# Another step order, other engines for some copies and other PSUM banks in a recurrent-attention and token-mixing kernel

## The chip, the cores and the metric

The kernel runs on one core of a Trainium2 chip. The time is device microseconds of one execution. Engines are named as in the profile: PE does matrix multiplies (PEld its weight loads), DVE, ACT and POOL work elementwise, SP issues the loads and stores. Each engine takes its instructions strictly in the order in which the program lists them, and an instruction waits until the steps that it depends on are done.

## The reference

Two stages follow each other. The first is a recurrence over 768 tokens, for 4 batches and 8 heads of width 48, with a decay `w` per token and channel; the second mixes the tokens of each batch by a matrix made from two projections, applies a relu and a last projection.

```python
for t in range(S):
    cur = np.einsum('bhd,bhe->bhde', u[None] * kt, vt)
    y[:, :, t] = np.einsum('bhd,bhde->bhe', rt, state + cur)
    state = wt[:, :, :, None] * state + np.einsum('bhd,bhe->bhde', kt, vt)
...
W_tok = scale * np.einsum('bsd,btd->bst', x @ w_q, x @ w_k)
mixed = np.einsum('bst,btd->bsd', W_tok, x)
return (np.maximum(mixed, 0.0) @ w_out).astype(np.float32)
```

Inputs and output are float32; `x` is the first stage's result, 4 x 768 x 384.

## The kernel before

The 3072 tokens are cut into 12 units of 256 (three to a batch), and each unit into two chunks of 128. Steps carry the unit's number and, where there are two, the chunk's: AM.8.1 is the second chunk of unit 8. A unit goes through these steps (in brackets the engines that may take one):

- Loads (SP): wg, kg, rg, vg, 384 KB each, into rings of four buffers; for the last batch v comes in four parts, vw. SP then also issues the stores, st.
- ln (ACT) takes the logarithm of the decay into lw, k16, r16 and v16 (POOL, ACT or DVE) cast k, r, v to bf16. On PE cw sums the logarithms along the tokens, kT and rT transpose k and r into one PSUM tile, vp reorders v. In PSUM they are read by ep and en (ACT: exponentials of the sum and of its negative), ks (a copy of the transposed k), VB (a copy of v; in the last batch straight from vw).
- RT (DVE) is r times ep, KT is k times en. KT has three forms: on POOL or DVE from the copy ks (way P or D, line 526), or on DVE straight from PSUM (way d, line 521). qT (DVE) is r times k; dps (PE) and dd make from it the current token's own share, and Vd (POOL or DVE, line 575) is VB times dd.
- A (PE) is the product of KT and RT per head, AM (DVE, line 595) masks it on its way out of PSUM. kb (PE) transposes KT back, kd copies it, sn (PE) forms the new state, SB (DVE) scales it. yi and ya (PE) give the output from the state and from AM and VB, and X (DVE, lines 710 and 715) adds Vd.
- xt, XT transpose X; qk and QK make the unit's queries and keys (in unit 11 they are split in wk, wq, wkc, wqc). When a batch is complete, T (PE) sums keys times X, TS copies it; then for each of the batch's units mx (PE), rl (relu into MX), fp (PE, the last projection), os (a copy out of PSUM) and st.

Units 0 and 11 do several steps in halves. Before unit 0, `setup` writes constants and masks and has PE do 18 multiplies of zeros, Z; twelve more such multiplies, z, lie among the steps. pads sets the unused columns of the two kd buffers to zero, uC, uT and UB bring the bonus `u` into place.

Nothing here is ordered by a scheduler. Class `Plan` only collects the 734 steps with their dependencies; `order` then reads three tables. `ORDER` (line 82) is a permutation of the steps' numbers: the program is written out in that order, and each engine gets its own steps in that order. `WAYS` (line 124) has a letter for each step that allows several, and picks the engine or the form; `BANKS` (line 129) gives the PSUM bank (of eight; a wide tile takes two) of each tile that lies there. A step that fills a bank waits until the bank's last reader is done.

```python
for s in self.steps:
    if len(s["ways"]) > 1:
        s["way"] = next(ways)
    s["eng"] = self.ENGINE[s["way"]]
for b, x in zip(self.banks, BANKS):
    b.bank = x
for i in ORDER:
    ...
```

Letters in `WAYS`: A, D and P are ACT, DVE and POOL, d is KT's PSUM form on DVE, and E, e and c are forms of a PE step: whole transposes or ones in 64-row halves, and a state product in two column halves (c).

Of the kernel before, what the change touches and what calls it, by code (L numbers as in the profile page):

```python
# [32 lines left out]
class Plan:  # L33
# [89 lines left out]
]  # L123
WAYS = (
    "PDDDAPPDDdPADPPDDEEEAAPPAdPAAPEAcEEAAPPAPPADPeDEEDAAAAAAAAPPDPDADPeAcEEDAPPAdPAAPEAEEEDA"
    "PPDPPAAPeAEEAAAAAAAAAAPDPPAAPEDEcEAAPPDPPDAPEAEEEAAPPDPPAAPeDceAAAAADADDPAAPPAPEDcEEDAPP"
    "DPPAPeAcceAAPPDPPPAPPAEEDDAEDADAAADAAAADADDA"
)
# [765 lines left out]
```

## Time and profile before

| | |
|---|---|
| runs | 100.68, 101.51, 102.75 us; median 101.51 |
| span of the profiled execution, first to last instruction | 99.6 us |
| instructions | 4492 |
| moved by DMA | 24.68 MB, mean 248 GB/s |
| granted PE clock | 1.00 |

The profiled execution's own time is its span and what lies before the first and after the last instruction; the trace shows only the span. The lowest of the three runs is 1.1 us over it, the median 1.9 us.

In a row of a timeline the first number is the start from the span's beginning, the second the time from the start of a group's first instruction to the end of its last, in us; brackets name the idle time of the engine before it and what ended that. In a row of the groups, `x8 | 17.4, 2169 | 2.3 <-` says eight instructions, 17.4 us busy, 2169 ns on average, 2.3 us of idle time before them and what ended it. Neighbours on one engine overlap by some 0.08 us, so means add up to a little more than busy time.

### The profile page before, as it was taken

Reading aid. Unit: us, or ns where it says so; the run is one execution under the profiler, and the core shown is the slowest. Engines: PE = TensorE matmul, PEld = TensorE weight load, DVE = VectorE, ACT = ScalarE, POOL = GpSimd, SP = SyncE. Lnnn points to the kernel's source line nnn. Section 1 sums busy time; section 2 is a strip of 40 time slices with the busy share of each in tenths; the row PEclk is TensorE's granted clock in tenths of the full one; section 3 lists DMA queues with packets and bytes.
Section 4 is the critical chain, followed back from the end, with each engine's and each line's share of the span. In section 5 each row is a group of like instructions: output and inputs, shape, how many; then the busy total and the mean of one; then the engine's idle time right before and its main releaser. Section 6 shows DMA issues by size and latency. Waiting matters only on the chain.

```text
span 99.6 us, 4492 instructions
## 1 busy us (share of the span) xinstructions
PE 86.6 (87%) x1906; PEld 63.3 (64%) x1911; DVE 84.9 (85%) x154; ACT 79.0 (79%) x135; POOL 69.5 (70%) x82
## 2 busy tenths in 40 slices
PE   5978796879886998999999999889998999999930
PEld 1325473756774767777776777759787687776610
DVE  6284999799979999979999999999999799783740
ACT  6034998799996799899999998999899766666920
POOL 6866354999799895799999989498996392500000
PEclk9999999999999999999999999999999999999999
DMA  1999999799999999999999977998993056030794
GB/s 17 313 327 349 324 337 296 195 295 335 289 314 298 225 311 329 344 321 268 271 330 305 316 114 218 251 156 201 282 417 115 7 210 264 10 158 7 277 367 149
DMA packets 45141, 24.68 MB, mean 248 GB/s; under 512 B 31552, under 2 KB 43968, under 8 KB 45120
## 3 DMA queue, kind: packets, MB, share of 16 engines
q1 hardware_dynamic: 44960, 24.19, 84.0%
q8 instruction: 15, 0.25, 0.9%
q10 hardware_dynamic: 160, 0.20, 0.5%
q14 instruction: 6, 0.05, 0.1%
HBM read 19.66 MB, written 4.72 MB: 245 GB/s over the span
## 4 chain that ended last, share of the span: by engine, by line
PE 37%; DVE 23%; SPq 20%; DMA 7%; issue 7%; ACT 3%; ACTq 0%; DVEq 0%
PE PS L179 37%; SPq L232 9%; SPq L237 8%; DMA vg<-in_v_dram 7%; DVE AM L595 7%; DVE X L710 6%; DVE RT L516 3%; SPq L355 2%; DVE qT L506 2%; DVE ks L333 2%; DVE SB L658 1%; ACT VB L327 1%; SPq L357 1%; ACT MX L339 1%; DVE kd L335 1%
## 5 line engine op out<-in xcount | busy, mean ns | idle before, releaser
L595 DVE TENSOR_TENSOR AM<-PS,US 128x1024 bf16<-128x1024 f32 x24 | 28.8, 1218 | 0.7 <-PE PS L179 0.7
L526 POOL TENSOR_TENSOR KT<-ks,en 128x1024 bf16<-128x1024 bf16 (+1 forms) x10 | 19.7, 1965 | 4.7 <-DVE ks L333 3.3
L575 POOL TENSOR_TENSOR Vd<-VB,dd 128x768 bf16<-128x768 bf16 (+1 forms) x14 | 18.1, 1293 | 4.5 <-ACT dd L327 3.4
L454 ACT ACTIVATE en<-PS 128x1024 bf16<-128x1024 f32 (+1 forms) x14 | 12.5, 907 | 3.0 <-PE PS L179 2.9
L179 PEld LDWEIGHTS <-KT 48*128 48x128 bf16 (+1 forms) x312 | 9.7, 94 | 6.6 <-issue 4.5
L447 ACT ACTIVATE ep<-PS 128x512 bf16<-128x512 f32 (+1 forms) x28 | 13.7, 555 | 0.1
L179 PE MATMUL PS<-wo,MX 128*128 128x384 bf16 x72 | 13.5, 327 | 0.0
L710 DVE SCALAR_TENSOR_TENSOR X<-PS,gx,Vd 128x384 bf16<-128x384 f32 x22 | 12.5, 609 | 0.7 <-PE PS L179 0.6
L407 ACT ACTIVATE lw<-wg 128x768 bf16<-128x768 f32 x12 | 10.3, 857 | 2.9 <-DMA wg<-in_w_dram 2.9
L179 PE MATMUL PS<-RT,KT 48*128 48x128 bf16 x192 | 9.7, 218 | 1.2 <-ACT VB L327 0.4
L327 ACT COPY os<-PS 128x768 f32<-128x768 f32 (+1 forms) x11 | 7.9, 714 | 3.5 <-PE PS L179 3.5
L418 POOL CAST k<-kg 128x768 bf16<-128x768 f32 x10 | 8.3, 827 | 2.5 <-DMA kg<-in_k_dram 2.5
L179 PE MATMUL PS<-Z 128*128 128x512 bf16 x25 | 8.4, 461 | 1.4 <-DVE Z L250 1.2
L418 POOL CAST r<-rg 128x768 bf16<-128x768 f32 x10 | 8.2, 825 | 1.6 <-DMA rg<-in_r_dram 1.6
L179 PEld LDWEIGHTS <-MX 128*128 128x128 bf16 x72 | 6.5, 97 | 3.6 <-DVE MX L341 0.2
L516 DVE TENSOR_TENSOR RT<-PS,ep 128x1024 bf16<-128x1024 bf16 (+1 forms) x14 | 8.4, 605 | 0.0
L179 PE MATMUL PS<-VB,AM 128*128 128x48 bf16 x192 | 8.0, 184 | 0.4 <-issue 0.4
L506 DVE TENSOR_TENSOR qT<-PS,ks 128x1024 bf16<-128x1024 bf16 x12 | 8.2, 684 | 0.1
L339 ACT ACTIVATE MX<-PS 128x768 bf16<-128x768 f32 (+1 forms) x12 | 8.0, 682 | 0.4
L179 PE MATMUL PS<-CM,lw 64*128 64x128 bf16 x192 | 7.4, 217 | 0.5 <-DVE AM L595 0.3
L327 ACT CAST VB<-PS 128x768 bf16<-128x768 f32 x8 | 6.4, 804 | 1.1 <-PE PS L179 0.6
L179 PEld LDWEIGHTS <-AM 128*128 128x128 bf16 x192 | 6.3, 96 | 1.6 <-issue 0.7
(90 smaller groups left out, 191.9 us busy)
## 6 DMA issues: line engine op xcount, KB each, us to landing
kg<-in_k_dram SPq DMA_DIRECT2D x12, 384.0 KB, 6.4
wg<-in_w_dram SPq DMA_DIRECT2D x12, 384.0 KB, 5.0
rg<-in_r_dram SPq DMA_DIRECT2D x12, 384.0 KB, 5.8
vg<-in_v_dram SPq DMA_DIRECT2D x9, 384.0 KB, 6.3
out_dram<-os SPq DMA_DIRECT2D x9, 384.0 KB, 2.5
vw<-in_v_dram SPq DMA_DIRECT2D x4, 288.0 KB, 6.7
out_dram<-os SPq DMA_DIRECT2D x5, 192.0 KB, 2.4
wof<-in_moe_w_out_dram SPq DMA_DIRECT2D x1, 576.0 KB, 6.2
```

The lines of the kernel that those rows point to most:

```text
L179: return nc.tensor.matmul(o, l, rr, start=start, stop=stop, skip_group_check=True, is_transpose=trans)
L327: nc.scalar.copy(o, i)
L407: nc.scalar.activation(view(lw.tile, 0, [[64, H], [512, 2], [1, D]]), view(g["wg"].tile, 0, [[D2, H], [D, 2], [1, D]]), ACT.Ln, bias=0.0, ...
L418: op(view(o.tile, 0, [[64, NP], [256, 4], [1, D]]), view(g[src].tile, 0, [[2 * D2, NP], [D, 4], [1, D]]))
L447: nc.scalar.activation(view(ep.tile, cs[0] * NP * EW + off, [[EW, NP * len(cs)], [step, 2], [1, 32]]), view(at(cw), cs[0] * 512 + j * 64, ...
L454: nc.scalar.activation(en.tile[:, ds(cs[0] * 512, w_)], at(cw)[:, ds(cs[0] * 512, w_)], ACT.Exp, bias=0.0, scale=-1.0)
L506: lambda e: nc.vector.tensor_tensor(plain(qT.tile), turned(512), plain(ks.tile), ALU.mult),
L516: nc.vector.tensor_tensor(plain(RT.tile, cs, 32), turned(512, cs, True), plain(ep.tile, cs, EW // 4), ALU.mult)
L526: x.tensor_tensor(KT.tile[:, cols], ks.tile[:, cols], en.tile[:, cols], ALU.mult)
L575: (nc.vector if e == "D" else nc.gpsimd).tensor_tensor(Vd.tile[:, cols], VB.tile[:, cols], view(dd.tile, cs[0] * H, [[1, len(cs) * H], [0, ...
L595: AMs[c] = add(("AM", n, c), "D", lambda e, c=c, A=A: nc.vector.tensor_tensor(view(AM[c].tile, 0, [[C, 8], [1, C]]), view(at(A), 0, [[C, 8 ...
L710: nc.vector.scalar_tensor_tensor(view(X.tile, 2 * i * DM + hh * D, [[D2, H], [1, D]]), view(at(y), hh * 512, [[D, H], [1, D]]), gx, view(V ...
```

## The change

All three tables are replaced; no other line is touched. Every step of before is there after, with the same dependencies.

```diff
 ORDER = [
-    0, 3, 13, 2, 21, 22, 23, 15, 16, 17, 1, 24, 25, 26, 27, 28, 29, 76, 77, 78, 31, 73, 74, 75,
+    0, 1, 2, 3, 4, 14, 13, 15, 16, 17, 18, 19, 30, 33, 73, 74, 75, 20, 85, 35, 37, 21, 22, 23,
...
 WAYS = (
-    "PDDDAPPDDdPADPPDDEEEAAPPAdPAAPEAcEEAAPPAPPADPeDEEDAAAAAAAAPPDPDADPeAcEEDAPPAdPAAPEAEEEDA"
+    "PPDADPPDdPPAAPPDDccEADPPAPAAAPEDcEEDAPPAdPADPEAceAAAAAAAAAPADPPADPeAEcEDAPPAdPAADeAEceDA"
...
 BANKS = [
-    7, 2, 0, 6, 0, 6, 4, 4, 1, 1, 6, 6, 5, 4, 2, 6, 0, 0, 0, 7, 7, 6, 4, 5, 4, 4, 2, 2, 7, 0, 0,
+    3, 0, 6, 0, 7, 4, 6, 0, 5, 4, 6, 4, 5, 4, 2, 6, 4, 6, 0, 5, 5, 6, 2, 4, 4, 2, 0, 2, 3, 0, 0,
...
```

Of the elementwise steps, these change their engine. To DVE: UB, QK.0, QK.10, XT.1, TS.8, TS.11, Vd.4, dd.6, dd.11, kd.1, kd.7, KT.2, KT.11 (both halves, in form d), wqc.11.0, os.6, os.9.1, and the relus rl.9 (both halves), rl.10.0 and rl.11.0. From DVE to ACT: uC, dd.0, XT.2, XT.9, XT.11.0, kd.2, kd.8, VB.7, ks.11, rl.7, rl.8, rl.11.1, os.8, os.9.0, os.10.1, os.11.0. Between POOL and the others: pads.0, KT.0.1, KT.1, v16.3, k16.6 and r16.9 come to POOL, v16.1 and r16.3 go from it to ACT. KT.0's first half stays on DVE and takes form d. On PE 18 steps change their form.

SP's first loads are wg.0, wg.1, kg.0, rg.0, kg.1, vg.0 in place of kg.0, wg.0, rg.0, vg.0, kg.1, wg.1; later wg.3 stands ahead of the weights, and vg.3 ahead of kg.4 and behind wg.4; wg.11 ahead of kg.11.

The first place is POOL's queue from its first cast on. Names are those of the buffers, so KT_0 and Vd_0 hold the even units. Before:

```order
L421 CAST k16_0_89<-kg_0_71 128x8x2x48
L421 CAST r16_0_87<-rg_0_67 128x8x2x48
L333 CAST v16_0_103<-vg_0_75 128x8x2x48
L418 CAST k16_1_90<-kg_1_72 128x4x4x48
L418 CAST r16_1_88<-rg_1_68 128x4x4x48
L333 CAST v16_1_104<-vg_1_76 128x8x2x48
L575 TENSOR_TENSOR Vd_0_109<-VB_0_105,dd_0_107 128x384
L418 CAST k16_0_89<-kg_2_73 128x4x4x48
L575 TENSOR_TENSOR Vd_0_109<-VB_0_105,dd_0_107 128x384
```

After:

```order
L297 MEMSET kd_0_83 128x64
L298 MEMSET kd_0_83 128x16x80
L421 CAST k16_0_89<-kg_0_71 128x8x2x48
L421 CAST r16_0_87<-rg_0_67 128x8x2x48
L526 TENSOR_TENSOR KT_0_101<-ks_0_95,en_0_93 128x512
L418 CAST k16_1_90<-kg_1_72 128x4x4x48
L333 CAST v16_0_103<-vg_0_75 128x8x2x48
L418 CAST r16_1_88<-rg_1_68 128x4x4x48
L526 TENSOR_TENSOR KT_1_102<-ks_1_96,en_1_94 128x1024
L575 TENSOR_TENSOR Vd_0_109<-VB_0_105,dd_0_107 128x384 x2
L418 CAST k16_0_89<-kg_2_73 128x4x4x48
```

A pad, half of KT.0 and all of KT.1 have come in; v16.1 has left; both halves of Vd.0 stand behind KT.1 and ahead of k16.2.

The second place is DVE's queue around the two steps that read only SBUF. Before, in unit 3, from the masked second chunk of unit 2 on:

```order
L595 TENSOR_TENSOR AM1_0_113<-PS_62,US_146 128x1024
L333 COPY ks_1_96<-PS_62 128x1024
L658 TENSOR_TENSOR SB_0_115<-PS_62,ep_0_91 128x192
L333 CAST v16_1_104<-vg_3_78 128x8x2x48
L506 TENSOR_TENSOR qT_1_98<-PS_62,ks_1_96 128x1024
L516 TENSOR_TENSOR RT_1_100<-PS_62,ep_1_92 128x1024
L710 SCALAR_TENSOR_TENSOR X_0_125<-PS_62,gx_150,Vd_0_109 128x8x48 x2
```

After, in unit 5, from ks.5 on:

```order
L333 COPY ks_1_96<-PS_62 128x1024
L506 TENSOR_TENSOR qT_1_98<-PS_62,ks_1_96 128x1024
L658 TENSOR_TENSOR SB_0_115<-PS_62,ep_0_91 128x192
L516 TENSOR_TENSOR RT_1_100<-PS_62,ep_1_92 128x1024
L575 TENSOR_TENSOR Vd_0_109<-VB_0_105,dd_0_107 128x768
L595 TENSOR_TENSOR AM0_0_111<-PS_62,US_146 128x1024
L595 TENSOR_TENSOR AM1_1_114<-PS_62,US_146 128x1024
```

The cast of v.3 has left DVE's queue; the product Vd.4, which was POOL's, stands ahead of the masks of units 4 and 5.

The third place is the end of DVE's queue, from the first half of X.11 on. Before:

```order
L715 SCALAR_TENSOR_TENSOR X_1_126<-PS_62,gx_150,Vd_1_110 128x384 x2
L333 COPY XT_1_120<-PS_62 128x384
L333 COPY XT_0_119<-PS_62 128x384
L333 CAST QK_1_128<-PS_62 128x64
L341 TENSOR_SCALAR MX_3_124<-PS_62 128x768
L341 TENSOR_SCALAR MX_0_121<-PS_62 128x768
L333 CAST QK_1_128<-PS_62 128x128
L333 COPY os_0_79<-PS_62 128x768
L333 COPY os_1_80<-PS_62 128x384
L341 TENSOR_SCALAR MX_3_124<-PS_62 128x3x128
L333 COPY os_2_81<-PS_62 128x384
L333 COPY os_3_82<-PS_62 128x384
```

After:

```order
L715 SCALAR_TENSOR_TENSOR X_1_126<-PS_62,gx_150,Vd_1_110 128x384
L333 COPY os_2_81<-PS_62 128x768
L715 SCALAR_TENSOR_TENSOR X_1_126<-PS_62,gx_150,Vd_1_110 128x384
L333 COPY XT_0_119<-PS_62 128x384
L333 CAST QK_1_128<-PS_62 128x64
L333 CAST QK_1_128<-PS_62 128x384
L333 CAST QK_1_128<-PS_62 128x128 x2
L333 CAST TS_1_130<-PS_62 128x384
L341 TENSOR_SCALAR MX_1_122<-PS_62 128x3x128
L341 TENSOR_SCALAR MX_2_123<-PS_62 128x3x128
L341 TENSOR_SCALAR MX_3_124<-PS_62 128x3x128
L341 TENSOR_SCALAR MX_1_122<-PS_62 128x3x128
```

os.6 stands between the halves of X.11, the relus of units 9 to 11 follow TS.11, and one more row, a copy os_1 of half of unit 9, ends the queue. On PE the order behind T.11 was fp.7, mx.9, fp.8, mx.10, fp.9, mx.11, fp.10, fp.11 and is fp.8, mx.9, mx.10, mx.11, fp.9.0, fp.10, fp.11, fp.9.1, with fp.7 ahead of T.11.

More of the change, by code (lines that the diff above doesn't have):

```diff
@@ L82 @@
 ORDER = [
[40 rows of a table removed]
[40 rows of a table added]
 ]
 WAYS = (
-    "PDDDAPPDDdPADPPDDEEEAAPPAdPAAPEAcEEAAPPAPPADPeDEEDAAAAAAAAPPDPDADPeAcEEDAPPAdPAAPEAEEEDA"
-    "PPDPPAAPeAEEAAAAAAAAAAPDPPAAPEDEcEAAPPDPPDAPEAEEEAAPPDPPAAPeDceAAAAADADDPAAPPAPEDcEEDAPP"
-    "DPPAPeAcceAAPPDPPPAPPAEEDDAEDADAAADAAAADADDA"
+    "PPDADPPDdPPAAPPDDccEADPPAPAAAPEDcEEDAPPAdPADPEAceAAAAAAAAAPADPPADPeAEcEDAPPAdPAADeAEceDA"
+    "PPDPPAAPeAcEAAAAAAAAAPPDPPADPEDEEeAAPPDPPAAPEDcEEAAPPDPPAAPEAceAADADAAAAPPAPPAPEDEEeAAPP"
+    "DPPAPeAEceADPPAddPDPPAEEADDEDADDDDADDAAADAAA"
 )
 BANKS = [
[6 rows of a table removed]
[6 rows of a table added]
 ]
```

88 rows, old and new, of tables (BANKS, ORDER) are left out of this document.

## The prediction

> **What bounds the kernel now.** I read the page's busy line first, then the chain of waits, then four stretches of the span cut at the places where the bound changes, and last the timelines of DVE, POOL and SP. The profiled execution spans 99.6 us; what lies around it is not in the trace. The runs are 100.68, 101.51 and 102.75 us, so the median stands 1.9 us over this span, and I add 1.9 us at the end.
>
> ```profile
> PE 86.6 (87%) x1906; PEld 63.3 (64%) x1911; DVE 84.9 (85%) x154; ACT 79.0 (79%) x135; POOL 69.5 (70%) x82
> PE 37%; DVE 23%; SPq 20%; DMA 7%; issue 7%; ACT 3%; ACTq 0%; DVEq 0%
> ```
>
> No engine is full over the whole span, and the chain changes hands: loads first, DVE in the middle, PE at the end. The stretches show where. The columns are PE, PEld, DVE, ACT, POOL busy us, granted clock, DMA share, GB/s.
>
> ```profile
> 8.52:33.38 24.86, 20.27 (x550) 15.39 (x547) 23.01 (x40) 21.58 (x36) 19.06 (x20) 1.00 1.04 296
> 33.38:68.24 34.86, 33.03 (x847) 25.32 (x840) 34.31 (x55) 34.00 (x55) 31.13 (x27) 1.00 1.02 268
> 68.24:87.40 19.16, 18.49 (x422) 14.56 (x419) 17.45 (x30) 15.12 (x29) 13.17 (x13) 1.00 0.54 187
> 87.40:99.60 12.20, 8.16 (x70) 5.33 (x67) 5.65 (x11) 5.88 (x14) 0.00 (x0) 1.00 0.52 195
> ```
>
> The cuts are DVE's: its first copy of unit 0 starts at 8.52, the last score mask of unit 8 (AM.8.1) ends at 65.89 + 2.35 = 68.24. In the first stretch DVE works 23.01 of 24.86 us, in the second 34.31 of 34.86. So from 8.52 to 68.24 DVE is the bound, with 1.85 + 0.55 = 2.40 us idle. DMA is full as well (1.04 and 1.02), and ACT has only 0.86 us free in the second stretch. The granted clock is 1.00 in all four, so it is no part of the argument.
>
> ```profile
> 8.52 0.69 DVE L333 COPY ks<-PS 128x1024 bf16<-128x1024 bf16 x1 [0.94 <-PE PS L179]
> 65.89 2.35 DVE L595 TENSOR_TENSOR AM<-PS,US 128x1024 bf16<-128x1024 f32 x2
> 67.17 9.67 PE PS L179 x260
> 85.56 10.02 PE PS L179 x107
> 95.64 0.48 ACT os L327
> ```
>
> From 67.17 the chain is PE's almost without a break, to 95.58; then ACT's last copy, the store and its landing, 4 us in all. What DVE waits for while it is the bound, by the longest waits (us in total, times, longest):
>
> ```profile
> DVE v L333 <- DMA vg<-in_v_dram: 0.7, 1, 0.7
> DVE X L710 <- PE PS L179: 0.6, 1, 0.6
> DVE KT L526 <- ACT en L454: 0.4, 1, 0.4
> ```
>
> **The change part by part.** The instructions stay the same in kind and nearly in number; ORDER, WAYS and BANKS decide the rest. I split the span at the start of ks.0, at the end of AM.8.1 and at the end of PE's work. This works because both versions have done the same set of DVE steps at AM.8.1 (units 0 to 8, all but their late copies), and PE has nearly the same list left after it, in nearly the same order.
>
> *The head, up to ks.0.*
>
> ```profile
> 5.46 0.84 ACT L407 ACTIVATE lw<-wg 128x768 bf16<-128x768 f32 x1 [2.92 <-DMA wg<-in_w_dram]
> 8.96 1.08 ACT L454 ACTIVATE en<-PS 128x512 bf16<-128x512 f32 x2 [2.66 <-PE PS L179]
> 1.23 5.73 PE L179 MATMUL PS<-Z 128*128 128x512 bf16 x18 [1.23 <-DVE Z L250]
> 8.32 0.61 PE L179 MATMUL PS<-CM,lw 64*128 64x128 bf16 x16
> ```
>
> The decay load was second on SP and is now first, so ln.0 can start before 5.46; but cw.0 cannot pass PE's 18 warming matmuls, which end at 1.23 + 5.73 = 6.96. It now stands ahead of kT.0 right behind them, and uC, for which PE waited there, is on ACT, ahead of ln.0. So cw.0 can start near 7.1 instead of 8.32, en.0 a cw later (0.61), near 7.7 instead of 8.96, and ks.0, behind kT.0, near 8.0 instead of 8.52. Against that, k.0 is now the third load and POOL sets a pad to zero ahead of its cast. I take 0.5 us sooner; between 1.2 sooner (all that cw.0 gains) and 0.8 later (one more POOL step of 0.83 that nothing covers).
>
> *DVE from ks.0 to AM.8.1.* The rows that price it:
>
> ```profile
> L521 DVE TENSOR_TENSOR KT<-PS,en 128x1024 bf16<-128x1024 bf16 x2 | 1.4, 678 | 0.0
> L521 DVE TENSOR_TENSOR KT<-PS,en 128x512 bf16<-128x512 bf16 x1 | 0.4, 411 | 0.0
> L333 DVE COPY XT<-PS 128x768 bf16<-128x768 bf16 x4 | 2.2, 550 | 0.0
> L333 DVE CAST VB<-PS 128x768 bf16<-128x768 f32 x1 | 0.9, 949 | 0.0
> L333 DVE COPY dd<-PS 128x16 f32<-128x16 f32 x3 | 0.5, 163 | 0.0
> L335 DVE TENSOR_SCALAR kd<-PS,gk 128x384 bf16<-128x384 bf16 x4 | 1.6, 410 | 0.0
> L335 DVE TENSOR_SCALAR kd<-PS,gk 128x768 bf16<-128x768 bf16 x2 | 1.2, 608 | 0.0
> L333 DVE COPY os<-PS 128x384 f32<-128x384 f32 x3 | 1.6, 549 | 0.0
> L333 DVE COPY os<-PS 128x768 f32<-128x768 f32 x1 | 1.0, 958 | 1.6 <-ACT MX L339 1.6
> L526 POOL TENSOR_TENSOR KT<-ks,en 128x1024 bf16<-128x1024 bf16 x8 | 17.4, 2169 | 2.3 <-ACT ep L447 1.1 <-DVE ks L333 0.8 <-ACT en L454 0.3
> L575 POOL TENSOR_TENSOR Vd<-VB,dd 128x384 bf16<-128x384 bf16 x4 | 3.3, 831 | 2.8 <-ACT dd L327 2.0 <-DVE dd L333 0.8
> L575 POOL TENSOR_TENSOR Vd<-VB,dd 128x768 bf16<-128x768 bf16 x10 | 14.8, 1478 | 1.8 <-ACT dd L327 1.4 <-DMA vg<-in_v_dram 0.3
> ```
>
> Gone from DVE: both halves of KT.0 (0.68 by its row below + 0.411), KT.1 (0.678), XT.2 (0.550), VB.7 (0.949), v16.3 (1.31, below), dd.0 (0.163), kd.2 and kd.8 (half width, 0.410 each): 5.56 us. New on it: half of KT.0 in its PSUM form (0.411), KT.2 (0.678), XT.1 (0.550), kd.1 and kd.7 (0.608 each), dd.6 (0.163), QK.0 (no such row on DVE; os of the same 128x384 f32 from PSUM, 0.549): 3.57 us, and Vd.4. Neighbours overlap by about 0.08 us, which nearly cancels (nine rows gone, eight new). So it is Vd.4 less 2.0 us.
>
> Vd.4 has no row on DVE. It reads two SBUF tiles, as did v16.3 (one) and the first KT half (two), and these show what happens beside POOL:
>
> ```profile
> 9.59 0.68 DVE L526 TENSOR_TENSOR KT<-ks,en 128x512 bf16<-128x512 bf16 x1 [0.38 <-ACT en L454]
> 9.17 0.83 POOL L418 CAST k<-kg 128x768 bf16<-128x768 f32 x1 [0.41 <-DMA kg<-in_k_dram]
> 28.62 1.31 DVE L333 CAST v<-vg 128x768 bf16<-128x768 f32 x1 [0.73 <-DMA vg<-in_v_dram]
> 28.04 1.48 POOL L575 TENSOR_TENSOR Vd<-VB,dd 128x768 bf16<-128x768 bf16 x1
> 29.47 2.44 POOL L526 TENSOR_TENSOR KT<-ks,en 128x1024 bf16<-128x1024 bf16 x1
> 11.55 0.83 POOL L418 CAST r<-rg 128x768 bf16<-128x768 f32 x1 [1.55 <-DMA rg<-in_r_dram]
> 19.32 1.14 DVE L710 SCALAR_TENSOR_TENSOR X<-PS,gx,Vd 128x384 bf16<-128x384 f32 x2 [0.62 <-PE PS L179]
> ```
>
> KT.0's first half ended at 10.27, 0.27 after POOL's cast ended (10.00); its PSUM twin of that size takes 0.411 with no such wait. v16.3 ended at 29.93, 0.41 after POOL's Vd (29.52), and POOL's next KT took 2.44 where the mean is 2.17. So such a DVE step seems to stand until POOL's running one ends. Vd.4 alone should take 0.5 (KT's PSUM form, 0.678 x 768/1024) to 0.95 (VB, the same 768 columns); beside POOL up to 2.17 more, if a KT has just begun there. I take 1.3, v16.3's row, as the nearest, and keep 0.5 and 3.1. DVE's work therefore shrinks by 0.7 (between 1.5 less and 1.1 more).
>
> The Trainium skill, in "SBUF — State Buffer", section "Who interferes with whom", says the pair of SBUF ports that DVE and GpSimd share is an exclusive lock for a whole instruction. By it Vd.4 waits for the whole of the POOL step that is running: with half of a KT left (1.08 us) it would take 1.6 to 2.0, and the sum would be 0.3 to 0.7 us worse. The trace agrees in the two places above (0.27 and 0.41 us after POOL's end).
>
> *DVE's idle time there*, 2.40 us. The wait of 0.73 for v.3 goes with v16.3, which moves to POOL, and vg.3 is now issued ahead of kg.4; the 0.38 at KT.0's first half goes too, as that half no longer stands behind POOL. What comes instead is not to be read from a trace of the old order. The place most at risk is X.0, which needs both Vd.0 halves, and these stand behind KT.1 on POOL now. POOL's r16.1 waits for its load to 11.55; with 0.83 for it, 2.17 for KT.1 and 2 x 0.83 for Vd.0 they are done near 16.2, and X.0 started at 19.32. POOL has 24.86 - 19.06 = 5.8 us free in that stretch, so unit 1 should not starve. I take 2.1 us idle, between 0.6 and 6.
>
> So AM.8.1 ends 0.5 + 0.7 + 0.3 = 1.5 us sooner.
>
> *PE's tail.* PE's list from kT.10 on is the same set, but for the form of xt.9 and of two sn steps; these forms I cost at nothing, on PE in the middle too, where DVE is the bound and covers them. KT.11 moves from POOL to DVE, ks.11 and XT.9 from DVE to ACT, TS.8, dd.11 and os.6 to DVE. On DVE that is 2 x 0.411 + 0.549 + 0.163 + 0.958 in, 0.678 (KT's PSUM form, for ks of the same 1024 columns) + 0.550 out: 1.26 us more in a stretch with 19.16 - 17.45 = 1.7 us free. os.6 stands between the two halves of X.11; xt.11.1 on PE waits for it, and its cover is what PE has in between: mx.7, ya.11.1, qk.9, xt.11.0, qk.10 and mx.8. If that cover failed it would cost up to os.6's 0.96 us.
>
> At the very end three mx now come before the six fp halves. The first fp half waits for a relu on DVE (0.55, by the os row of that shape) that the other two mx mostly hide: 0.1 us, between 0 and 0.55. The last copy goes from ACT to DVE (0.55 for 0.48): 0.1 more. The tail is 0.2 us longer.
>
> **Sum.** 99.6 - 1.5 + 0.2 = 98.3 us of span, and with 1.9 around it 100.2 us.
>
> **The rivals.** *The queues close up.* DVE's idle falls to 0.6 us (the second stretch shows 0.55 in 35 us), Vd.4 costs 0.5, the head gains its 1.2: 1.2 + 1.5 + 1.8 = 4.5 us at AM.8.1. POOL then caps it: it has 34.86 - 31.13 = 3.7 us free in the second stretch and as many steps there as before. That gives 99.6 - 3.7 + 0.2 + 1.9 = 98.0 us, and 97.2 without the cap. For it: two of the three longest waits lose their cause. Against it: three terms have to come out at their best ends together.
>
> *The lead is lost at the end.*
>
> ```profile
> 67.87 1.69 SPq L237 DMA_DIRECT2D rg<-in_r_dram  x1
> rg<-in_r_dram SPq DMA_DIRECT2D x12, 384.0 KB, 5.8
> 74.80 0.83 POOL L418 CAST r<-rg 128x768 bf16<-128x768 f32 x1
> ```
>
> DMA is at 1.02 to 1.04 and moves the same bytes; the last r load, issued at 67.87, lands near 73.7 by its 5.8 us. If DMA gains nothing, unit 11 starts where it did, whatever DVE gained. Then 99.6 + 0.2 + 1.9 = 101.7 us. For it: the share. Against it: r.11's cast ran at 74.80, 1.1 us after the landing, and kg.6 and wg.11 now stand earlier on SP.
>
> *ACT becomes the bound, and the kernel slower.* r16.3 and v16.1 are on ACT now, and r16.3 stands behind kd.2, which waits for kb.2 on PE, which waits for KT.2 on DVE; behind it are en.3, ln.4 and ep.3, and PE's rT.3 holds all its later steps. From there ACT has to stay ahead. In the first stretch ACT idles 24.86 - 21.58 = 3.28 us, 13%, in the second 0.86, 2.5%. If these crossings keep the second stretch at 13%, it grows by 34.86 x 0.13 - 0.86 = 3.7 us; with the head's and the work's gains of 1.2 and the tail's 0.2 the span is 99.6 + 3.7 - 1.2 + 0.2 = 102.3, and 104.2 us. It decides once ACT idles above some 2 us between 33 and 68. For it: ACT's 0.86 us leave no room. Against it: between those cuts ACT gives up k16.6, r16.9, dd.6 and kd.7 and takes VB.7, XT.2 and half a kd, so it has no more to do there.
>
> **How the numbers follow.** The forecast gets 0.36 (99.2 to 101.2 by itself), the closed queues 0.25, the lost lead 0.20, ACT 0.19. A measurement of this kernel can tell about 2% from no change, 2.0 us, as its three runs lie that far apart. Faster by over 2% means under 99.5: 0.22 of the closed queues and 0.09 of the forecast's lower edge, 0.31. Slower means over 103.5: 0.15 of ACT, and 0.03 for the dear ends of DVE's terms (6 us idle, Vd.4 at 3.1) in the other cases, 0.18. The rest, 0.51, is within 2%. The range goes down to 97.5, between the closed queues' two prices, and up to 103.6, which leaves out most of ACT's case: some 0.04 below and 0.16 above.
>
> **What would show it.** Right: DVE's AM.8.1 (the 18th and last mask of unit 8) ends near 66.7, DVE idles near 2 us before it, Vd on DVE takes 1 to 1.6 us, and PE runs unbroken from there to near 94.5. en.0 starts near 7.7. Wrong: a new wait of over 1 us on DVE between 10 and 35 us (POOL's KT or ACT's r), ACT idle by over 2 us between 33 and 68, PE waiting for r.11 near 74, or PE gaps after the last T.

## The result, and the profile after

The changed kernel takes 108.94 us in the median (107.83 to 110.02, four runs), the kernel before on the same chip 101.72 us (100.68 to 102.75): the ratio is 1.065, with a 95% interval of 1.055 to 1.075. Forecast were 100.2 us and a range of 97.5 to 103.6. Ratios are taken over undisturbed runs, so they need not be the quotient of two medians.

The page of the changed kernel, its span, the busy line, the row of the granted PE clock in 40 slices of 2.65 us, and the shares of the chain:

```profile
span 106.1 us, 4548 instructions
PE 90.0 (85%) x1937; PEld 65.2 (61%) x1939; DVE 84.8 (80%) x154; ACT 80.8 (76%) x134; POOL 69.1 (65%) x83
PEclk9999999955799999958999999999999999999999
PE 45%; DVE 26%; ACT 9%; issue 6%; DMA 5%; POOL 4%; SPq 2%; DVEq 0%; POOLq 0%; ACTq 0%
```

DVE has as much to do as before (84.8 us for 84.9), but the span is 6.5 us longer. PE is busy for 3.4 us more with nearly the same list, and the clock row says why: in two places, near 22 to 27 us and 45 to 48, it was granted half its clock. Before, all forty digits were 9.

The stretches, cut at ks.0, the first mask of unit 3, AM.8.1 and the end of X.11 as before, but the second cut lies at the end of that mask (35.12 us), where before it lay at its start (33.38); so of the first two stretches only the sum is compared:

```profile
9.22:35.12 25.90, 21.36 (x516) 15.79 (x512) 22.75 (x39) 20.16 (x32) 20.00 (x21) 0.87 1.01 284
35.12:74.21 39.09, 34.31 (x876) 25.98 (x867) 35.21 (x55) 33.01 (x55) 30.81 (x27) 0.96 1.06 282
74.21:93.60 19.39, 18.96 (x429) 14.96 (x427) 18.58 (x32) 16.21 (x28) 11.54 (x11) 1.00 0.17 64
93.60:106.10 12.50, 8.16 (x65) 5.04 (x62) 4.51 (x12) 6.13 (x13) 0.00 (x0) 1.00 0.59 222
```

```profile
71.86 2.35 DVE L595 TENSOR_TENSOR AM<-PS,US 128x1024 bf16<-128x1024 f32 x2
99.55 2.60 PE L179 MATMUL PS<-wo,MX 128*128 128x384 bf16 x15 [0.32 <-ACT MX L339]
```

AM.8.1 ends at 71.86 + 2.35 = 74.21 us, 5.97 later than before, and not 1.5 sooner; behind it come 31.9 us where there were 31.4. From ks.0 to AM.8.1 it is 64.99 us for 59.72. DVE works 22.75 + 35.21 = 57.96 of them (57.31 before) and idles 7.03 (2.40 before). The starts of X, the output of each unit, show in which units the time was lost:

| start, us | ks.0 | X.0 | X.1 | X.2 | X.3 | X.4 | X.5 | X.6 | X.8 |
|---|---|---|---|---|---|---|---|---|---|
| before | 8.52 | 19.32 | 24.42 | 31.05 | 37.44 | 45.38 | 49.75 | 58.49 | 68.78 |
| after | 9.22 | 18.35 | 26.96 | 31.64 | 39.71 | 50.67 | 55.17 | 63.39 | 74.75 |

X.0 comes 1.0 us sooner. Then X.0 to X.1 takes 3.5 us more than before, X.2 to X.3 1.7 more and X.3 to X.4 3.0 more; X.1 to X.2 takes 2.0 less. In each of the three longer gaps stands one wait of one kind. On PE, where all of its later steps stand behind it, with the copies that it waits for:

```profile
19.20 1.01 ACT L327 COPY ks<-PS 128x1024 bf16<-128x1024 bf16 x1
20.26 0.41 PE L179 MATMUL PS<-PM,r 64*128 64x64 bf16 x16 [1.10 <-ACT ks L327]
42.62 0.69 DVE L333 COPY ks<-PS 128x1024 bf16<-128x1024 bf16 x1
43.36 0.41 PE L179 MATMUL PS<-PM,r 64*128 64x64 bf16 x16 [1.33 <-DVE ks L333]
```

`PS<-PM,r` is the transpose rT, of unit 2 and of unit 5. It does not use the copy ks; what it needs, r, is long there. But kT and rT of a unit lie in one PSUM tile, in the same two banks, and ks is read out of it. Steps that touch a bank wait for each other in the order of `ORDER`, whether or not they touch the same columns. Before, rT.5 stood ahead of ks.5, and rT.2 stood eleven steps behind ks.2 in `ORDER`; now ks.2 and ks.5 stand close ahead of rT.2 and rT.5 (two steps and one), and PE waits for 1.10 and 1.33 us until ACT has finished one copy (19.20 + 1.01) and DVE the other (42.62 + 0.69).

The same on DVE, with the order the other way round:

```profile
9.22 0.69 DVE L333 COPY ks<-PS 128x1024 bf16<-128x1024 bf16 x1 [2.29 <-PE PS L179]
36.51 0.69 DVE L521 TENSOR_TENSOR KT<-PS,en 128x1024 bf16<-128x1024 bf16 x1 [1.13 <-ACT ks L327]
```

ks.0, now behind rT.0, waits until PE has also transposed r.0. KT.4, which reads PSUM itself, now stands behind ks.4 and waits for ACT's copy, though both only read.

And behind each of the two stops of PE the clock falls (columns as in the stretches, the clock is the third number from the end):

```profile
21.00:22.00 1.00, 1.00 (x19) 0.61 (x18) 1.00 (x3) 0.25 (x2) 0.75 (x1) 0.52 0.84 193
22.00:27.00 5.00, 4.78 (x72) 3.45 (x70) 3.50 (x6) 3.51 (x5) 3.17 (x4) 0.50 1.08 316
27.00:28.00 1.00, 1.00 (x24) 0.80 (x22) 1.00 (x2) 0.14 (x2) 1.00 (x2) 0.57 1.16 321
45.00:48.00 3.00, 3.00 (x31) 2.06 (x30) 2.59 (x4) 2.21 (x6) 3.00 (x4) 0.50 0.93 235
```

By the shares of half and full clock in the first and the last of such slices, PE runs at 0.50 from 21.0 to 27.9 us and from 44.9 to 48.3, and is busy nearly all of that time (4.78 of 5.00 us, 3.00 of 3.00).

### The profile page after: what moved, and what is told of

Read it like the earlier page. It is cut to its first block, busy times and chain, and to the rows that moved or that the text cites. A ratio compares the mean times of both kernels' runs of the same rounds, so it can differ in the third digit from the quotient of the medians.

```text
span 106.1 us, 4548 instructions
## 1 busy us (share of the span) xinstructions
PE 90.0 (85%) x1937; PEld 65.2 (61%) x1939; DVE 84.8 (80%) x154; ACT 80.8 (76%) x134; POOL 69.1 (65%) x83
## 4 chain that ended last, share of the span: by engine, by line
PE 45%; DVE 26%; ACT 9%; issue 6%; DMA 5%; POOL 4%; SPq 2%; DVEq 0%; POOLq 0%; ACTq 0%
PE PS L179 45%; DVE AM L595 8%; DMA rg<-in_r_dram 5%; ACT ks L327 4%; DVE RT L516 3%; DVE ks L333 3%; DVE X L710 3%; DVE qT L506 2%; DVE SB L658 2%; SPq L232 2%; ACT os L327 1%; POOL KT L526 1%; DVE MX L341 1%; DVE XT L333 1%; ACT kd L329 1%
## 5 line engine op out<-in xcount | busy, mean ns | idle before, releaser
L526 POOL TENSOR_TENSOR KT<-ks,en 128x1024 bf16<-128x1024 bf16 (+1 forms) x9 | 18.1, 2021 | 9.4 <-DVE ks L333 9.1
L575 POOL TENSOR_TENSOR Vd<-VB,dd 128x768 bf16<-128x768 bf16 (+1 forms) x13 | 16.5, 1279 | 10.0 <-DVE dd L333 6.8
L179 PEld LDWEIGHTS <-KT 48*128 48x128 bf16 (+1 forms) x312 | 10.4, 97 | 6.8 <-issue 2.9
L179 PE MATMUL PS<-wo,MX 128*128 128x384 bf16 x72 | 14.0, 334 | 0.5 <-ACT MX L339 0.3
L179 PE MATMUL PS<-RT,KT 48*128 48x128 bf16 x192 | 10.4, 228 | 0.4 <-DVE SB L658 0.2
L179 PE MATMUL PS<-Z 128*128 128x512 bf16 x28 | 9.6, 456 | 1.5 <-DVE Z L250 1.2
L327 ACT COPY os<-PS 128x768 f32<-128x768 f32 (+1 forms) x13 | 8.7, 680 | 2.2 <-PE PS L179 2.2
L418 POOL CAST k<-kg 128x768 bf16<-128x768 f32 x11 | 9.8, 892 | 0.3 <-POOL Vd L575 0.3
L327 ACT CAST VB<-PS 128x768 bf16<-128x768 f32 x9 | 7.2, 802 | 1.3 <-PE PS L179 1.2
L327 ACT COPY XT<-PS 128x768 bf16<-128x768 bf16 (+1 forms) x9 | 6.9, 763 | 1.6 <-PE PS L179 1.4
```

The costliest lines, as they stand in the source:

```text
L179: return nc.tensor.matmul(o, l, rr, start=start, stop=stop, skip_group_check=True, is_transpose=trans)
L327: nc.scalar.copy(o, i)
L418: op(view(o.tile, 0, [[64, NP], [256, 4], [1, D]]), view(g[src].tile, 0, [[2 * D2, NP], [D, 4], [1, D]]))
L526: x.tensor_tensor(KT.tile[:, cols], ks.tile[:, cols], en.tile[:, cols], ALU.mult)
L575: (nc.vector if e == "D" else nc.gpsimd).tensor_tensor(Vd.tile[:, cols], VB.tile[:, cols], view(dd.tile, cs[0] * H, [[1, len(cs) * H], [0, ...
```

## The experiments

Theory A: the bank waits at rT.2 and rT.5, with the half clock behind them, are most of the loss. Theory B: the waits are, and the clock is a symptom without price. Theory C: no single wait matters, the new order of the queues is worse as a whole. `ORDER` holds numbers of steps; the first experiments move single numbers so that each engine's queue stays exactly as it was, and only who waits for whom at a bank turns round.

**Two copies behind their transposes** (ks.2 is 142 and rT.2 141, ks.5 309 and rT.5 308).

```diff
+for a, b in ((142, 141), (309, 308)):
+    ORDER.remove(a); ORDER.insert(ORDER.index(b) + 1, a)
```

> The changed kernel with two steps moved in the list: the copies ks.2 and ks.5 now stand behind the transposes rT.2 and rT.5 instead of ahead of them. The queue of every engine stays word for word the same; only who waits for whom in the PSUM bank that kT, rT and ks share is turned round. Theory A (PE's two stops at rT, 1.10 and 1.33 us, and the half clock that follows each, 10 us in all, cost most of the 6.5): both stops and both stretches of half clock are gone, mean clock 1.00, 103 us (102 to 104.5). Theory B (the stops alone; PE is not the bound there, so its clock costs nothing): 106.5 us (105.5 to 107). Theory C (the whole order of the queues is worse, these two places are no more than its signs): 107 us or more, the stops turn up elsewhere.

Measured: 105.47 us (104.04 to 105.89), ratio 1.031 (1.024 to 1.039): 3.5 of the 7.2 us in the medians, with two steps moved in the order and no queue changed. C falls as the whole answer. It came out between A and B. The clock row of its profile:

```profile
PEclk9999995799999999999999999999999999999999
```

Both falls of the changed kernel are gone, but there is another, shorter one, earlier. Two of its four executions had it by their mean clock (0.98), two were at 1.00.

**One of the two alone**, ks.5 behind rT.5.

```diff
+for a, b in ((309, 308),):
+    ORDER.remove(a); ORDER.insert(ORDER.index(b) + 1, a)
```

> The changed kernel with one copy alone put back behind its transposes: ks.5 behind rT.5; ks.2 still stands ahead of rT.2. Both together took 3.5 us off the changed kernel's 108.9. If the two stops cost about the same: 107.2 us, and the trace shows PE's stop of about 1.1 us at rT.2 near 20 us and none at rT.5 near 43. If the stop at rT.5 is the dear one, since it is the longer (1.33 us) and the clock stayed at half for some 4 us behind it: 106.0 us. If nearly all lay at rT.2: 108.5 us.

Measured: 107.0 us (105.75 to 108.57), ratio 1.046 (1.031 to 1.060). That is 1.9 us for ks.5 and 1.5 for ks.2 in the medians: about the same each, within the runs' spread. PE's stop at rT.2 is still there, and so of the same size:

```profile
22.15 0.41 PE L179 MATMUL PS<-PM,r 64*128 64x64 bf16 x16 [1.10 <-ACT ks L327]
```

**The clock alone.** The waits stay; behind kT.2 and kT.5, where PE is about to stop, it multiplies zeros into a bank that is free then.

```diff
+FILL = {140: 5, 307: 6}
     if s["fn"] is not None:
         s["fn"](s["way"])
+    for _ in range(FILL.get(s["i"], 0)):
+        mm(PS[:, ds(7 * 512, 512)], Z[:, ds(0, C)], Z)
```

> The changed kernel with its waits as they are, but PE multiplies zeros while it would stand: 5 multiplies of 512 columns behind kT.2 and 6 behind kT.5, about 1.1 and 1.3 us of PE work in a bank that is free there. Theory A (the half clock costs most): the clock stays at 1.00 in both places although the waits remain, 104.5 us (103 to 106). Theory B (the waits alone): 108 us or a little more. Theory C (the order as a whole): 108 us.

Measured: 106.85 us (106.71 to 108.75), ratio 1.053 (1.051 to 1.056). The clock behind the second stop, and the row over the span:

```profile
PEclk9999995799999999999999999999999999999999
46.00:48.00 2.00, 2.00 (x40) 1.29 (x38) 2.00 (x2) 2.00 (x5) 2.00 (x2) 1.00 0.90 238
```

No fall is left at 22 or 45 us, and the time is 2.1 us less in the medians, 1.1% by the ratios, with PE having eleven multiplies more to do. By their mean clock (0.96 to 0.98) all four executions have a short early fall like the one in the row, which the eleven multiplies don't touch, so these figures are rather too small for the two.

The traces separate the clock from the waits. From X.0 to X.5, behind any early fall, it takes 36.82 us as changed, 34.08 with the multiplies (no half clock, PE still held up), 32.49 with the two copies moved (neither), and 30.43 before. So in this stretch the half clock cost 2.7 us and the two stops 1.6, by one execution of each; B falls. Not all of these 4.3 us arrive at the end: the spans of the changed kernel and of the one with two copies are 2.0 us apart, the latter having an early fall of its own.

**The other way round in the kernel before**: ks.5 ahead of rT.5, every queue as it was.

```diff
+for a, b in ((309, 307),):
+    ORDER.remove(a); ORDER.insert(ORDER.index(b) + 1, a)
```

> The kernel before with one step moved in the list: the copy ks.5 now stands ahead of the transpose rT.5, as in the changed kernel; every engine's queue stays the same. Theory A: PE stops at rT.5 for about 1 us until DVE's copy is done, the clock falls to half for some 3 us behind it if the stop is long enough, and the time rises by 1.5 to 4 us, to 103 to 105.5. Theory B: the stop alone, 0.5 to 1.3 us more, 102 to 103. Theory C: no measurable difference, 101.5.

Measured: 103.58 us (102.23 to 104.69), ratio 1.012 (1.006 to 1.018): 2.1 us in the medians, 1.2% by the ratio. The stop and the clock behind it, in the slowest of the four executions:

```profile
41.51 0.61 PE L179 MATMUL PS<-PM,r 64*128 64x64 bf16 x16 [1.32 <-DVE ks L333]
42.00:44.00 2.00, 2.00 (x26) 1.36 (x22) 0.90 (x3) 0.09 (x1) 2.00 (x2) 0.50 1.09 324
PEclk9999975599999999589999999999999999999999
```

One moved number makes the same stop (1.32 us) in the old order, and here the same fall; X.3 to X.4 takes 10.19 us for 7.94. But one of the four executions had a mean clock of 1.00 and took 102.23 us, so this order does not always bring the fall. The row shows an early fall too, at 14 to 20 us, ahead of anything that the edit touches; more on that below.

**Four copies**: the two above, ks.0 ahead of rT.0, and ks.4 behind KT.4.

```diff
+for a, b in ((142, 141), (309, 308), (40, 32), (260, 263)):
+    ORDER.remove(a); ORDER.insert(ORDER.index(b) + 1, a)
```

> The changed kernel with four copies moved in the list and every queue unchanged: ks.2 and ks.5 behind rT.2 and rT.5, ks.0 ahead of rT.0 (it stood 1.3 us behind kT.0 for it), ks.4 behind KT.4, which waited 1.13 us for it. Theory A: as with the first two alone, and up to 1.5 us less, 101.5 to 103. Theory B: 0.5 to 1.5 us less than with the first two alone. Theory C: 107 us or more.

Measured: 104.23 us (103.02 to 105.00), ratio 1.031 (1.024 to 1.038). Against two copies that is 1.2 us in the medians, and nothing by the ratios (1.031 for both); the medians mix executions with and without an early fall. The profiled execution has none:

```profile
span 101.3 us, 4550 instructions
PEclk9999999999999999999999999999999999999999
8.54 0.69 DVE L333 COPY ks<-PS 128x1024 bf16<-128x1024 bf16 x1 [0.63 <-PE PS L179]
34.86 0.41 PE L179 MATMUL PS<-PM,r 64*128 64x64 bf16 x16 [0.62 <-ACT ks L327]
```

ks.0 starts at 8.54 instead of 9.22, the span is 101.3 us: 4.8 less than after's, 1.7 more than before's. From ks.0 to AM.8.1 DVE works 57.53 us and idles 3.32, for 7.03 as changed. A's 101.5 to 103 was too low. One reason stands in the last row: before, rT.4 was ahead of ks.4; here ks.4 is behind KT.4 but still ahead of rT.4, and PE waits 0.62 us for it, a new stop of the old kind.

**Vd.4 back on POOL**, on top of the four copies, by its letter in `WAYS`, `D` before.

```diff
+WAYS = list(WAYS); WAYS[80] = 'P'
```

> The changed kernel with four copies set right (104.23 us) and the step Vd.4 back on POOL instead of DVE, at the same place in the order. On DVE it took 1.58 us. If DVE is the bound there and POOL has room: 102.7 us. If the DVE time only fills a stall that comes later: 104.2 us. If POOL is then late with KT.5 and the casts behind it: 104.8 us or more.

Measured: 104.41 us (103.48 to 105.28), ratio 1.023 (1.012 to 1.034) for 1.031 (1.024 to 1.038) with the four copies alone. No gain in the median, and the intervals overlap. Taking the 1.58 us off DVE gave it waits for the same unit instead:

```profile
43.14 1.23 DVE L595 TENSOR_TENSOR AM<-PS,US 128x1024 bf16<-128x1024 f32 x1 [0.41 <-PE PS L179]
44.65 1.22 DVE L595 TENSOR_TENSOR AM<-PS,US 128x1024 bf16<-128x1024 f32 x1 [0.29 <-ACT lw L407]
46.42 1.14 DVE L710 SCALAR_TENSOR_TENSOR X<-PS,gx,Vd 128x384 bf16<-128x384 f32 x2 [0.55 <-POOL Vd L575]
```

X.3 to X.4 is 46.42 - 37.54 = 8.88 us, and with Vd.4 on DVE it was 45.78 - 36.90 = 8.88 us too.

**One part of the change alone, on the kernel before**: the cast of v.3 on POOL, by its letter, `D` before.

```diff
+WAYS = list(WAYS); WAYS[62] = 'P'
```

> The kernel before with one part of the change alone: the cast of v.3 on POOL instead of DVE, at the same place in the order. On DVE it took 1.31 us behind a wait of 0.73 us for its load. If DVE's list is the bound and POOL has room, as the prediction reckoned: 1.3 to 2.0 us less than before, 99.5 to 100.2 us. If POOL, which is held by the same load, is then late with KT.3 and Vd.2: 101.5 us or a little more.

Measured: 102.04 us (100.58 to 103.77, ten runs), ratio 0.999 (0.992 to 1.006). Before, X.2 and X.3 start at 31.05 and 37.44 us; here, with POOL's and PE's rows between them:

```profile
30.05 1.14 DVE L710 SCALAR_TENSOR_TENSOR X<-PS,gx,Vd 128x384 bf16<-128x384 f32 x2 [0.71 <-PE PS L179]
29.39 0.82 POOL L333 CAST v<-vg 128x768 bf16<-128x768 f32 x1
30.18 2.12 POOL L526 TENSOR_TENSOR KT<-ks,en 128x1024 bf16<-128x1024 bf16 x1
32.36 0.37 PE L179 MATMUL PS<-ID,KT 48*128 48x48 bf16 x16 [0.59 <-POOL KT L526]
33.07 1.22 DVE L595 TENSOR_TENSOR AM<-PS,US 128x1024 bf16<-128x1024 f32 x1 [0.61 <-PE PS L179]
37.42 1.13 DVE L710 SCALAR_TENSOR_TENSOR X<-PS,gx,Vd 128x384 bf16<-128x384 f32 x2
```

DVE lost 1.31 us of work and a wait of 0.73 us. One us of that arrives at X.2. But POOL now casts v.3 ahead of KT.3, which starts at 30.18 instead of 29.47; PE waits for KT.3, DVE's next mask for PE, and X.3 starts where it did, within 0.02 us. So the work that the prediction counted off DVE is not worth its length, even in the old order.

**The old end**, on top of the four copies: X.11.1 ahead of os.6, and the 43 steps from mx.9 on in the old order, with the old engines (and those of TS.11 and os.8). It is not the whole old end: fp.8, os.7 and os.8 stay ahead of mx.9, and KT.11, ks.11, XT.9, XT.11 and rl.8 keep their new engines.

```diff
+for a, b in ((142, 141), (309, 308), (40, 32), (260, 263), (674, 520), (685, 684), (686, 685),
...
+    ORDER.remove(a); ORDER.insert(ORDER.index(b) + 1, a)
+WAYS = list(WAYS); WAYS[208] = 'A'; WAYS[209] = 'A'; WAYS[212] = 'A'; WAYS[210] = 'D'; WAYS[211] = 'A'
...
```

> The changed kernel with four copies set right (104.23 us) and in addition the end of the program as it was before: the gated output X.11.1 ahead of the output copy os.6, and the steps from mx.9 on in the old order with the old engines. In the trace of the kernel with four copies the way from the end of DVE's last score mask to the end is 14.66 us, against 14.03 before. If this order costs what it seems: 0.6 us less, 103.6 us, and the way is 14.0. If the end is set elsewhere (PE has the same work in either order): 104.2 us.

Measured: 103.96 us (102.87 to 104.36), ratio 1.020 (1.010 to 1.030). The median is 0.3 us down, the ratio 1.1%, with overlapping intervals, but the trace does not bear the theory out: from the last mask to the end it takes 102.5 - (85.62 + 2.35) = 14.53 us, for 14.66 with the new end and 14.03 before. PE waits for 0.39 and 0.26 us among its last steps there, for a copy and a relu on DVE, where before it has no wait; what makes these two late is not found.

This run holds an accident that is worth more than its purpose. Up to the first half of X.11 it is the same program as the one with four copies, but its profiled execution had a fall of the clock. X.0 and X.1 and the clock between them, first with four copies, then with the old end:

```profile
18.34 1.14 DVE L710 SCALAR_TENSOR_TENSOR X<-PS,gx,Vd 128x384 bf16<-128x384 f32 x2 [0.17 <-PE PS L179]
24.95 1.14 DVE L710 SCALAR_TENSOR_TENSOR X<-PS,gx,Vd 128x384 bf16<-128x384 f32 x2
22.00:25.00 3.00, 2.65 (x67) 2.04 (x67) 2.96 (x5) 2.45 (x4) 1.16 (x2) 1.00 1.07 316
```

```profile
18.16 1.14 DVE L710 SCALAR_TENSOR_TENSOR X<-PS,gx,Vd 128x384 bf16<-128x384 f32 x2 [0.17 <-PE PS L179]
25.90 1.14 DVE L710 SCALAR_TENSOR_TENSOR X<-PS,gx,Vd 128x384 bf16<-128x384 f32 x2 [0.56 <-PE PS L179]
22.00:25.00 3.00, 2.78 (x31) 1.81 (x32) 2.57 (x4) 1.54 (x2) 1.10 (x1) 0.53 1.06 308
```

7.74 us for 6.61: 3.4 us at half the clock cost 1.1 us, and nothing in the program is different up to there.

**Three more places**, on top of that: ks.2 also behind RT.2, rT.9 right behind kT.9, r16.9 on ACT as before, behind VB.7.

```diff
+for a, b in ((554, 553), (549, 433), (142, 144)):
+    ORDER.remove(a); ORDER.insert(ORDER.index(b) + 1, a)
+WAYS = list(WAYS); WAYS[161] = 'A'
```

> The changed kernel with four copies set right and the old end (103.96 us), and three more places of the order: ks.2 also behind RT.2 (RT.2 on DVE waited 0.67 us for that copy), rT.9 right behind kT.9, ahead of cw.9, and r16.9 on ACT as before, behind VB.7 (ks.9 on ACT waited 0.94 us for rT.9, and DVE's qT.9 0.70 us for ks.9). If what is left of the loss is the sum of such waits for one place in the order: 1.2 us less or a little more, 102.7 us, and the mask AM.8.1 ends 1.0 to 1.4 us sooner. If the waits only move on to the next transfer or engine, as they did when Vd.4 went back to POOL: 104.0 us.

Measured: 104.34 us (102.98 to 106.48, six runs), ratio 1.024 (1.015 to 1.033). The waits only moved:

```profile
20.27 1.01 ACT L327 COPY ks<-PS 128x1024 bf16<-128x1024 bf16 x1 [1.33 <-DVE RT L516]
21.32 0.69 DVE L506 TENSOR_TENSOR qT<-PS,ks 128x1024 bf16<-128x1024 bf16 x1 [0.79 <-ACT ks L327]
58.50 0.62 DVE L335 TENSOR_SCALAR kd<-PS,gk 128x768 bf16<-128x768 bf16 x1 [0.71 <-PE PS L179]
```

RT.2 no longer waits for ks.2; ks.2 waits 1.33 us for RT.2, and qT.2, which needs the copy, 0.79. The 0.70 us at unit 9 came back as 0.71 at a kd. The profiled span is 101.3 us again.

**The same with three multiplies of zeros** behind rT.2, near 20 us.

```diff
+FILL = {141: 3}
```

> The kernel with the three more places set right, and three multiplies of zeros on PE behind rT.2, in a bank that nothing else uses then, so that PE idles less near 20 us, where the granted clock fell to 0.5 in one of two executions that are alike up to there (X.1 then came 0.95 us later). If that fall costs what it seems and the multiplies keep it away: the same as the kernel without them in an execution without a fall, and about 0.7 us less in the median, 102.0 us. If the fall is soaked up later, or the multiplies only delay PE: 102.7 us or up to 0.6 us more.

Measured: 103.03 us (102.68 to 103.42), ratio 1.013 (1.007 to 1.020): 1.3 us less in the median than without them, from three instructions that compute nothing. By the ratios it is 1.1%, and the intervals overlap, so the gain is likely and not proved. The mean clock of its four executions is 0.99 to 1.00; of the six without the multiplies it was 0.99 once, and 0.97 to 0.98 five times, with spans of 101.3 and of 102.4 to 104.8 us. PE does them where it waited:

```profile
19.13 0.81 PE L179 MATMUL PS<-Z 128*128 128x512 bf16 x3 [0.20 <-DVE X L710]
```

**The same idea on the kernel before**: seven multiplies at four places between 11 and 21 us.

```diff
+FILL = {91: 1, 100: 1, 105: 2, 141: 3}
+    for _ in range(FILL.get(s["i"], 0)):
+        mm(PS[:, ds(3 * 512, 512)], Z[:, ds(0, C)], Z)
```

Some of them write over the second chunk's transposes of units 1 and 2, so that part of the output is not the reference's; the work is the same.

> The kernel before with seven more multiplies of zeros on PE, in a bank that no step uses then, at four places between 11 and 21 us where PE waits anyway (one each behind kT.1 and dps.1, two behind A.1.1, three behind rT.2). The mean granted clock of the kernel before lay between 0.95 and 1.00 over its executions, so it falls in some of them too. If a fall costs here what it cost in the changed order (1.3 us in the median): the clock is 0.99 to 1.00 in every execution and the time 0.4 to 0.8 us below before, 101.0 us. If the loads, which keep the DMA engines full until 68 us, soak the loss up, as they soaked up what v.3 on POOL gained: the clock is steady and the time the same, 101.6 us.

Measured: 101.41 us (100.74 to 102.97, twelve runs) against 102.18 for before beside it, ratio 0.997 (0.992 to 1.001). The clock is 0.98 to 1.00 in all twelve; before's executions lay between 0.95 and 1.00. A gain of up to 0.8% is possible and not proved. **With v.3's cast on POOL as well** (`WAYS[62] = 'P'`):

> The same with the cast of v.3 on POOL instead of DVE as well. That cast alone on POOL gained 1.0 us at X.2 and nothing at X.3. If the falls of the clock had hidden its gain in the median: 0.5 us below the kernel with the multiplies alone, 100.5 us. If its gain ends at X.3, as that trace shows: the same as with the multiplies alone, 101.0 to 101.6 us.

Measured: 102.18 us (100.84 to 104.22, twelve runs), ratio 1.003 (0.998 to 1.009), with the same part overwritten. No gain from the cast, as its own trace had said. Three of these twelve executions have a mean clock of only 0.97 to 0.98, so the multiplies do not always keep it up. None of the kernels beats before by what a measurement can tell.

Put together, in medians: 108.94 us as changed; 105.47 with two copies set right, 104.23 with four; 103.03 with the old end, three more places and a steady clock. Before stands at 101.5 to 102.2 over the sets of runs (101.73 beside the last of these). About 1.3 us is left, of which some 0.5 lies in the end.

Where the rest lies can be read from the execution with four copies and no fall. Its X.2 starts at 29.32 us, 1.7 ahead of before; X.4 at 45.78, 0.4 behind; X.6 at 58.56, 0.1 behind; X.7 at 65.13, 1.15 behind, for 63.98 before. So 2.1 us go between X.2 and X.4, where PE stops at rT.4, and 1.1 between X.6 and X.7, where DVE's qT.9 waits 0.70 us for ks.9. With the three more places X.6 to X.7 takes 0.8 less, but X.5 to X.6 0.7 more. What the stop at rT.4 is worth was not tried, and neither were the new `BANKS`, the order of the loads and most of the new engines by themselves.

## Why the prediction was wrong

*"DVE's idle time ... I take 2.1 us idle, between 0.6 and 6."* This is the step that failed: 7.03 us, outside its own range. In the terms of the sum, the head came 0.70 us later (0.5 sooner forecast), DVE's work 0.65 more (0.7 less), its idle time 4.63 more (0.3 less), the tail 0.53 more (0.2 more). Of the 7.03 us, 4.3 end with a step of PE, which stood at rT.2 and rT.5 until a copy out of the same bank was done and ran at half its clock behind that; 1.1 more are KT.4's behind ks.4. With the four copies moved the idle time is 3.32 us, within the range. The prediction said that what comes is not to be read from a trace of the old order, and looked only at transfers and at POOL. Three of the four new waits could be looked for in `ORDER` itself, without a trace: which of ks and rT of a unit, and which of ks and KT, comes first changes at units 0, 4 and 5. That alone does not give the price: at units 3 and 8 the pair of ks and rT turns round too, and nothing waits there, and at unit 2 it does not turn, ks.2 only moves from eleven steps ahead of rT.2 to two. The old trace held a row of the kind, rT.1 waiting for the copy ks.1, which it does not use; it was not quoted, since it is 0.19 us:

```profile
13.76 0.41 PE L179 MATMUL PS<-PM,r 64*128 64x64 bf16 x16 [0.19 <-ACT ks L327]
```

The Trainium skill, "PSUM — Partial Sum Buffer", section "PSUM bank collisions raise a hardware error", says that the compiler adds a dependency between any two instructions of different engines that touch the same bank in the same 32 partitions, reads alike, and that a different address does not help. The traces agree: rT.2 waited 1.10 us for a copy of other columns, and KT.4 1.13 us for another reader.

*"The granted clock is 1.00 in all four, so it is no part of the argument."* Wrong in the conclusion. A 1.00 measured in one order says nothing of another, and this order made PE stop for over 1 us at two places. The half clock behind them cost 2.7 us from X.0 to X.5, and PE's length was treated as fixed all through.

*"DVE's work therefore shrinks by 0.7."* By busy time it grew by 0.65 (57.31 to 57.96), and by 0.22 with the four copies (57.53). Vd.4 took 1.58 us for the 1.3 assumed, inside its range; a wait ends the overlap of neighbours, which the sum took as constant (the steps' own lengths add up to 64.35 us for 64.57). But the larger fault is the premise "from 8.52 to 68.24 DVE is the bound". It idled for only 2.40 us, yet PE, POOL and ACT were so close behind that 2.0 us less for DVE moved nothing behind X.3, and 1.58 us less nothing at X.4.

```profile
45.52 2.32 POOL L418 CAST k<-kg 128x768 bf16<-128x768 f32 x2
45.58 1.58 DVE L575 TENSOR_TENSOR Vd<-VB,dd 128x768 bf16<-128x768 bf16 x1
```

POOL's two casts of k (0.83 us each, some 1.6 together) took 2.32 beside Vd.4, and Vd.4 ended at 47.16, ahead of the second one's end at 47.84. This agrees with the exclusive port of the prediction's citation: the first cast runs its 0.83 us, Vd.4 ends 0.8 behind it, and the second cast, begun at 46.29, takes 1.56. The 1.6 us that the citation gave was the better figure, though it was reckoned for half a KT on POOL, and casts stood there.

*The head, 0.5 us sooner.* The first half held: en.0 starts at 7.32 us (7.7 forecast).

```profile
7.32 1.08 ACT L454 ACTIVATE en<-PS 128x512 bf16<-128x512 f32 x2 [0.42 <-PE PS L179]
```

ks.0 then came at 9.22 instead of 8.0, since it had been placed "behind kT.0", and stood behind rT.0 as well. With that one turned round it was 7.87 to 8.54 in five traces. X.0's lead of 1.0 us was gone by X.1.

*The tail, 0.2 us longer.* 0.5 measured. The first fp half starts right behind the three mx, which hid DVE's relu as forecast. The wait of 0.32 us in the row further up is that of the next one, fp.10, for a relu on ACT, which the prediction did not name; the rest is not settled.

*The rivals.* "Slower" had 0.18, and one mechanism, ACT. ACT did idle by more than 2 us in its stretch (39.09 - 33.01 = 6.1), but as a follower of PE, whose steps end 4.8 us of these waits: its named chain, r16.3 behind kd.2 and rT.3 behind that, held nothing up, and rT.3 had no wait at all. The closed queues and the lost lead never came into play. ACT's case came nearest, as it had PE held up at an rT, but at rT.3 and for its data; no rival had PE stop for a bank that a copy is reading.

## What to carry to other kernels

Where an order table decides which of two engines touches a PSUM bank first, list for every shared tile the order of writer and readers, before and after; a pair that turns round, or comes close together, can be a wait that the old trace does not show. When one engine is "the bound" at 98%, ask of each us taken off it which engine is next, and by how much. And where a new order makes PE stop, reckon with a price for the clock behind it as well (here 2.7 us for the 1.6 of the stops), also where the old trace shows full clock.

## What the runs showed of the hardware

In the changed kernel stops of PE of 1.10 and 1.33 us, ending at 20.26 and 43.36, were followed by a granted clock of 0.50 from 21.0 and 44.9 us on. It stayed there for 6.8 us and 3.4 us, in the run with the old end for 3.4, and for 6.8 in the early fall of the kernel before with ks.5 first. PE's busy time in the 3.40 us ahead of these falls, in the same order:

```profile
17.64:21.04 3.40, 2.30 (x78) 1.83 (x75) 2.37 (x6) 2.48 (x5) 1.98 (x3) 1.00 0.80 205
41.54:44.94 3.40, 2.07 (x65) 1.62 (x61) 2.69 (x6) 1.91 (x4) 1.49 (x1) 1.00 1.09 313
```

```profile
18.02:21.42 3.40, 2.32 (x72) 1.80 (x71) 2.58 (x6) 2.74 (x4) 2.40 (x3) 1.00 0.53 119
```

```profile
10.54:13.94 3.40, 2.81 (x77) 2.01 (x77) 3.25 (x7) 3.40 (x8) 1.66 (x2) 1.00 1.15 328
```

And a stretch of the four copies with no fall in it or behind it:

```profile
19.80:23.20 3.40, 2.15 (x40) 1.65 (x42) 2.78 (x5) 2.35 (x5) 1.48 (x1) 1.00 0.75 224
```

A fall came behind 2.07, 2.30 and 2.32 us of 3.40, but once also behind 2.81, and none behind 2.15 in another execution. So PE's busy time by these records does not tell a fall by itself, and one program has executions with and without one. The Trainium skill, "TensorE: Matmul & The Clock Gate", section "Part 1: The HAM clock gate (the "warmup" mystery)", tells of a window of about 3.4 us that runs freely, and of the half clock after an idle window. The lengths of once and twice 3.4 us agree with the window, and a window that runs freely would explain the chance. That the window has to be idle does not agree: PE was busy for 61% or more of the 3.40 us ahead of each fall.

How much of the array is in use orders the falls better. In all 14 traces the stretches between two changes of the clock are whole multiples of 3.41 us. Cut each trace into these windows, and in each add up the multiplies, every one weighted by its columns and by the share of the 128x128 array that it fills, so that a 128*128 multiply of 512 columns counts 1. The ten falls come behind sums of 4.8 to 6.0. Of the other 363 windows at full clock only two lie as low, with 4.9 (the kernel before) and 5.1 (four copies), in traces that lack the records of 5 and 2 of the 30 multiplies of zeros; the next has 6.1. Of the twelve windows at half clock the two lowest, 5.0 and 5.2, are those behind which it stayed at half. So it seems to matter how little of the array a window fills, and where the window starts, which differs between executions: 17.62 us as changed, 18.01 with the old end, 19.60 with four copies. No run was made to test this.

In the kernel before the mean clock lay between 0.95 and 1.00 over its executions. Of its last 23 runs one took 248.6 us, at a clock of 1.00 and for no reason that is on record; of the other 22 the eleven with 0.99 or more have a median of 101.6 us, the other eleven one of 102.6.
